# The last 64 channels of a channel product as 64-row tiles of the TensorE array

## The chip, the cores and the metric

The kernel runs on one core of one Trainium2 chip. The metric is the device time of one execution in microseconds (us), lower is better. TensorE is called PE below, VectorE DVE, ScalarE ACT, as in the profile's rows.

## What is computed

The reference first forms a small causal weighted sum over seven neighbours of each sequence position, with softmax weights per head, and then a mixer of two products: one over the sequence (tokens) and one over the channels. The part that the change touches is the channel part, at its end:

```
x   = weighted sum of 7 taps                       # [8, 4096, 192]
h   = relu(x.T @ w_tok1) @ w_tok2                  # token mixing
u   = x + h.T
out = u + relu(u @ w_ch1) @ w_ch2                  # 192 -> 1536 -> 192 channels
```

There are 8 batches of 4096 positions with 192 channels. `x` and the softmax weights arrive in single precision, the four mixer weights in double, and the result is single precision.

## The kernel before

The 32768 positions are worked in 64 groups of N = 512 positions, eight groups to a batch. A group `g` passes through `u` (positions as partitions), is transposed to channels as partitions, and then goes through six steps `p` of the channel part, each of which handles 256 of the 1536 features.

**Precision by two parts.** A single-precision factor is split into a rounded part (`hi`) and the rest (`lo`), and a product is formed as hi x hi + lo x hi + hi x lo in a fast one-pass format. The 192 channels are the rows of the first channel product `u @ w_ch1`. 128 of them (the `a` part) fill all rows of the array and need three matmuls: `w1a_hi` with `a_hi`, `w1a_lo` with `a_hi`, `w1a_hi` with `a_lo`. The last 64 (the `c` part) are stacked: the tile `uc` holds the rounded part in rows 0 to 63 and the rest in rows 64 to 127, and `w1c_hi` and `w1c_lo` hold the same 64 rows of weights twice. Two matmuls (L496) do the `c` part of one block of 128 features. So `channel1` issues, for each of the two feature blocks `j` of a step, five matmuls of 512 columns into one bank of `ph`.

**One step.** `channel1(g, p)` issues those ten matmuls, then `nc.scalar.activation` (L499, ACT) writes the rounded relu to `h`, and `scalar_tensor_tensor` (L500, DVE) its rest. `channel2` issues sixteen matmuls (L514, L516) on the `h` of two steps earlier, which accumulate over the six steps. `ph` shares a pool of two buffers (`ps_w`) with the results of the token matmuls `th` and `up`, so a `channel1` waits until the L500 of an earlier step has read its buffer.

**What stands between.** Within the steps of group `g` the kernel places the token matmuls of a later group (`do_token1`) and those that make `u` of group `g + 1` (`do_token2`, in two halves). After the second half, `columns_of` turns `u` around: one DVE transpose of 32 x 32 blocks (L468), 24 ACT copies of 32 rows each (L476) into `a_f` and `c_f`, and then `split_u`: ACT writes `a_hi` and rows 0 to 63 of `uc`, DVE subtracts for `a_lo` (L426) and for rows 64 to 127 of `uc` (L429). When the last of these has been issued, `ut[g + 1]` is set and the group may begin.

**What sets the order.** Each engine's queue is in the order in which the Python code issues. DVE and ACT have other work beside: the weighted sum (`attention`, L200 and L208, 13 DVE operations per group until the last batch), the softmax, and in the first batches the conversion of weights. This work stands in chains of items, each with a kind and a cost in ns. `pump` picks the next item with a small planner clock for each engine (`at`). A "v" item goes to DVE when its chain's due time allows, and of two that could start, a later chain is preferred only if it starts over 100 ns earlier. After a "v" item its chain waits 130 ns (`AFTER`), so that an item of another chain gets in between. "u" items (the copies of `columns_of` and `split_u`) go first, but only if they end by `max(at["pe"], w_at[0]) + C1 + LATE`. `C1` and `C2` are the planner's prices for `channel1` and `channel2` on PE, `TOP` that of L499. A chain is strictly serial: an item that may not be issued holds up all items behind it. If `ut[g + 1]` isn't set at the end of a group, `need` issues what is left and moves the planner's PE clock on by 500 ns a time.

**Start.** A prologue of 130 us converts the weights of the channel part and the first token weights from double precision and does the first batch's taps. The conversion of the `c` weights (`convert_channel`, which "w1c") splits them into a scratch tile `prk` and then makes eight ACT copies of 64 rows x 768 (L369) to write both halves of `w1c_hi` and `w1c_lo`.

Of the kernel before, what the change touches and what calls it, by code (L numbers as in the profile page):

```python
# [12 lines left out]
F32 = mybir.dt.float32  # L13
F32R = mybir.dt.float32r
# [7 lines left out]
def mixer_kernel(ctx: ExitStack, tc: tile.TileContext, x, wg, wt1, wt2, wc1, wc2, out):  # L22
    nc = tc.nc
    B, S, D = x.shape
# [20 lines left out]
    const = ctx.enter_context(tc.tile_pool(name="const", bufs=1))  # L45
# [12 lines left out]

    w1a_hi = const.tile([P, F], F32R, name="w1a_hi")
    w1a_lo = const.tile([P, F], F32R, name="w1a_lo")  # L60
    w1c_hi = const.tile([P, F], F32R, name="w1c_hi")
    w1c_lo = const.tile([P, F], F32R, name="w1c_lo")
    w2s = const.tile([P, NF, 2 * D], F32R, name="w2s")
    s0 = dram.tile([NCH, P, CT * R], F32, name="s0")
    s1 = dram.tile([NCH, P, CT * 2 * R], F32, name="s1")
# [42 lines left out]
    def raw_tile():  # L108

        n = staged["raw"]  # L110
        staged["raw"] += 1
        if pro is not None and n % 3 == 0:
            return pro.tile([P, NV, 2], U32, tag="raw", name="raw")
        tag = "w1" if (n - n // 3 - 1 if pro is not None else n + 1) % 2 else "raw"
        return p1.tile([P, NV, 2], U32, tag=tag, name="raw")
# [13 lines left out]
    def convert(raw, n, out):  # L129

        yield "gate", 0, lambda: state["vals"] < 2
        state["vals"] += 1
        v = val_tile()[:, 0:n]
        out.append(v)
        bits = v.bitcast(U32)
        low, high = raw[:, 0:n, 0], raw[:, 0:n, 1]
        act, stt = nc.scalar.activation, nc.vector.scalar_tensor_tensor
        yield "s", 950, lambda: act(v, high.bitcast(F32), AF.Abs)
        yield "s", 1050, lambda: act(v, v, AF.Sign, bias=below[:, 0:1])
        yield "s", 950, lambda: act(v, v, AF.Relu, scale=LOW30)  # L140
        cost = 70 + n * 1.05
        yield "v", cost, lambda: stt(bits, high, 3, bits, op0=ALU.logical_shift_left, op1=ALU.bitwise_and)
        yield "v", cost, lambda: stt(bits, low, 29, bits, op0=ALU.logical_shift_right, op1=ALU.bitwise_or)
        yield "v", cost, lambda: stt(bits, high, 0xC0000000, bits, op0=ALU.bitwise_and, op1=ALU.bitwise_or)

    def split(hi, lo, v):

        n = v.free_size()
        yield "a", 190 + n * 0.75, lambda: nc.scalar.copy(hi, v)
        yield "v", 70 + n * 1.05, lambda: nc.vector.tensor_sub(lo, v, hi.bitcast(F32))  # L150
# [81 lines left out]
    KA = 4  # L232
# [98 lines left out]
    HF = F // 2  # L331
    NF2 = NF // 3

    def fetch_channel(which, n):
        raw = raw_tile()
        if which == "w1a":
            cs = slice(2 * n * HF, 2 * (n + 1) * HF)
            nc.sync.dma_start(raw[:, 0:HF, :].rearrange("p n l -> p (n l)"), wc1[0:DA, cs])
        elif which == "w1c":
            for j in range(2):  # L340
                cs = slice(2 * j * HF, 2 * (j + 1) * HF)
                nc.sync.dma_start(raw[j * DC:(j + 1) * DC, 0:HF, :].rearrange("p n l -> p (n l)"), wc1[DA:D, cs])
        else:
            nc.sync.dma_start(
                raw[:, 0:NF2 * D, :].rearrange("p (f d) l -> p f (d l)", f=NF2),
                wc2[n * NF2 * P:(n + 1) * NF2 * P].rearrange("(f p) d -> p f d", p=P),
            )
        rawt[which, n] = raw

    def convert_channel(which, n, pool=None):  # L350
        out = []
        yield from convert(rawt.pop((which, n)), NF2 * D if which == "c2" else HF, out)
        yield "n", 0, lambda: raw_free()
        v, = out
        if which == "w1a":
            cs = slice(n * HF, (n + 1) * HF)
            yield from split(w1a_hi[:, cs], w1a_lo[:, cs], v)
        elif which == "c2":
            fs = slice(n * NF2, (n + 1) * NF2)
            yield from split(w2s[:, fs, 0:D], w2s[:, fs, D:2 * D], v.rearrange("p (f d) -> p f d", f=NF2))  # L360
        else:
            two = pool.tile([P, KA, CT, D], F32, tag="pr", name="prk", bufs=3)
            two = two.rearrange("p k t d -> p (k t d)").bitcast(F32R)
            hi, lo = two[:, 0:HF], two[:, HF:2 * HF]
            yield from split(hi, lo, v)
            for src, dst in ((hi, w1c_hi), (lo, w1c_lo)):
                for j in range(2):
                    for at in (0, DC):
                        yield "a", 730, lambda src=src, dst=dst, j=j, at=at: nc.scalar.copy(  # L369
                            dst[at:at + DC, j * HF:(j + 1) * HF], src[j * DC:(j + 1) * DC, :].bitcast(F32))  # L370

        def last():
            state["vals"] -= 1
            done.add((which, n))
        yield "n", 0, last
# [42 lines left out]
    ut = {}  # L418

    def split_u(m, a_f, c_f):  # L420
        a_hi = late.tile([P, N], F32R, tag="a_hi", name="a_hi", bufs=2)
        a_lo = late.tile([P, N], F32R, tag="a_lo", name="a_lo", bufs=2)
        uc = late.tile([P, N], F32R, tag="uc", name="uc", bufs=2)
        yield "u", 520, lambda: nc.scalar.copy(a_hi, a_f)  # L424
        yield "u", 520, lambda: nc.scalar.copy(uc[0:DC], c_f[0:DC])
        yield "v", 540, lambda: nc.vector.tensor_sub(a_lo, a_f, a_hi.bitcast(F32))  # L426

        def last():
            nc.vector.tensor_sub(uc[DC:P], c_f[0:DC], uc[0:DC].bitcast(F32))  # L429
            ut[m] = (a_hi, a_lo, uc)  # L430
        yield "v", 540, last

    Q = 32
    NQ = P // Q
# [52 lines left out]

    def channel1(g, p):

        a_hi, a_lo, uc = ut[g]  # L490
        ph = ps_w.tile([P, 2, 512], F32, tag="w", name="ph")
        steps = ((w1a_hi, a_hi), (w1a_lo, a_hi), (w1a_hi, a_lo), (w1c_hi, uc), (w1c_lo, uc))
        for j in range(2):
            fs = slice((2 * p + j) * P, (2 * p + j + 1) * P)
            for n, (w, u) in enumerate(steps):
                nc.tensor.matmul(ph[:, j, :], w[:, fs], u, start=n == 0, stop=n == len(steps) - 1)  # L496
        h = late.tile([P, 2, 2, N], F32R, tag="h", name="h", bufs=3)
        ht[g, p] = h
        nc.scalar.activation(h[:, :, 0, :], ph, AF.Relu)  # L499
        nc.vector.scalar_tensor_tensor(  # L500
            h[:, :, 1, :], ph, 0.0, h[:, :, 0, :].bitcast(F32), op0=ALU.max, op1=ALU.subtract
        )
# [32 lines left out]
    at = {"pe": 0.0, "act": 0.0, "dve": 0.0}  # L535
# [6 lines left out]
    SLACK_M = 400  # L542
    LATE = 300
    FIRST = 0
    C1, C2 = 2290, 2264
    TOP, LOW = 1040, 1135
    h_at, w_at, h1_at = {}, deque([0.0, 0.0]), {0: 0.0}
    free = {"acc": 0.0, "u": 0.0}
# [92 lines left out]
    def raw_free():  # L641

        if state["jobs"]:
            job, *what = state["jobs"].popleft()
            fetch_w2(*what) if job is convert_w2 else fetch_channel(*what)
            add_chain(job(*what), max(at["pe"], at["dve"]) + LOAD if at["pe"] > 0 else SOON)
# [29 lines left out]
    with tc.tile_pool(name="pro", bufs=1) as pro:  # L676
# [29 lines left out]
        for m in range(NCH):  # L706
# [3 lines left out]
            v, = w1_v.pop(m)  # L710
            current, channel = channel, None
            if m in between:
                fetch_channel(*between[m])
                channel = start(convert_channel(*between[m], pro))
            if m + 2 < NCH:
                start_w1(m + 2)
            elif m + 2 == NCH:
                fetch_w2(0)
                w2_it = start(convert_w2(0))
            else:  # L720
                fetch_channel("c2", 1)
                channel = start(convert_channel("c2", 1))
                fetch_channel("w1a", 1)
# [23 lines left out]
    late = ctx.enter_context(tc.tile_pool(name="late", bufs=1))  # L747
# [122 lines left out]
```

## Time and profile before

| | |
|---|---|
| median of 3 runs | 2344.61 us (2344.28 to 2345.2) |
| the profiled execution | 2343.91 us |
| its span in the profile | 2342.1 us |
| mean granted PE clock | 0.978 |

The profile is that of one execution. Its rows give the start and the length of instructions in us; a matmul's length includes the time in which its last columns pass through the array, so successive matmuls overlap in the rows and the step from one start to the next tells the pace. "Windows" are rows that give the busy time of each engine within a stretch of the span; a number in brackets after a row of the timeline is the idle time of the engine before it and what ended that. The lines themselves stand in the prediction.

### The profile page before, as it was taken

To read this page: it belongs to the slowest core of one execution; us is meant where nothing else is said; L and a number is where in the kernel's file an instruction comes from. 1 tells how busy PE (TensorE), PEld (TensorE's weight loads), DVE (VectorE), ACT (ScalarE), POOL (GpSimd) and SP (SyncE) were. 2 spreads that over 40 slices of the span, in tenths; PEclk is the share of its full clock that TensorE was granted. 3 is DMA by queue.
4 is the path that set the end of the run, shared out by engine and by line. 5 is a ranking of instruction groups with operands and counts; after the bars stand their busy time and mean duration, and the time that the engine had idled before them with its cause. 6 is when DMAs were issued, how large, how long until landed. Compare 5 with 4: busy or idle time off the path is not lost.

```text
span 2342.1 us, 30675 instructions
## 1 busy us (share of the span) xinstructions
PE 2196.7 (94%) x12256; PEld 1962.0 (84%) x12256; DVE 1842.1 (79%) x2231; ACT 1085.0 (46%) x2265; POOL 58.4 (2%) x104
## 2 busy tenths in 40 slices
PE   7869989999998999999999999999999999999998
PEld 5558878888887888888888888888888888899997
DVE  8889887878876888879887888869887798844443
ACT  4675443544534355345434434444443454344443
POOL 0000000000000000000000000000000000000000
PEclk9989999999999999999999999999999999999999
DMA  7733131223241333313332232332233132211110
GB/s 282 233 133 140 63 106 70 100 97 114 92 156 62 108 113 135 120 64 124 123 107 99 105 122 80 116 112 104 101 107 120 63 124 103 73 55 46 46 42 21
DMA packets 52127, 244.69 MB, mean 104 GB/s; under 512 B 6008, under 2 KB 15736, under 8 KB 38672
## 3 DMA queue, kind: packets, MB, share of 16 engines
q1 hardware_dynamic: 43360, 196.58, 24.3%
q0 software_dynamic: 8624, 46.14, 4.9%
q8 instruction: 97, 1.59, 0.3%
q14 instruction: 46, 0.38, 0.0%
HBM read 192.36 MB, written 50.33 MB: 104 GB/s over the span
## 4 chain that ended last, share of the span: by engine, by line
PE 38%; ACT 19%; DVE 14%; issue 11%; DMA 1%; POOL 0%; POOLq 0%; ACTq 0%; SPq 0%; DVEq 0%
PE ph L496 17%; ACT a_f L476 9%; PE acc L514 9%; ACT c_f L476 4%; PE acc L516 4%; ACT h L499 4%; DVE h L500 3%; DVE xa L208 3%; PE th L397 3%; DVE pr L200 3%; PE up L449 2%; DVE uc L429 1%; PE th L398 1%; DVE a_lo L426 1%; DMA w<-s 1%
## 5 line engine op out<-in xcount | busy, mean ns | idle before, releaser
L514 PE MATMUL acc<-w2s,h 128*128 128x384 f32 x3072 | 902.1, 358 | 0.0
L499 ACT ACTIVATE h<-ph 128x1024 fp32r<-128x1024 f32 x384 | 392.8, 1023 | 1004.4 <-PE ph L496 980.3
L516 PE MATMUL acc<-w2s,h 128*128 128x192 f32 x3072 | 773.5, 252 | 0.0
L500 DVE SCALAR_TENSOR_TENSOR h<-ph,h 128x1024 fp32r<-128x1024 f32 x384 | 468.3, 1220 | 294.3 <-ACT h L499 292.7
L516 PEld LDWEIGHTS acc<-w2s,h 128*128 128x128 f32 x3072 | 591.3, 192 | 16.0
L514 PEld LDWEIGHTS acc<-w2s,h 128*128 128x128 f32 x3072 | 583.3, 190 | 16.0
L496 PE MATMUL ph<-a_hi,w1a_hi 128*128 128x512 f32 x768 | 321.6, 419 | 58.9 <-ACT a_hi L424 33.9
L496 PE MATMUL ph<-uc,w1c_hi 128*128 128x512 f32 x768 | 311.7, 406 | 44.2 <-DVE uc L429 44.2
L200 DVE TENSOR_TENSOR pr<-xt,wn 128x768 f32<-128x768 f32 x336 | 318.2, 952 | 4.1
L208 DVE TENSOR_TENSOR xa<-xa,pr 128x768 f32<-128x768 f32 x336 | 319.7, 952 | 1.0
L496 PE MATMUL ph<-a_lo,w1a_hi 128*128 128x512 f32 x768 | 306.8, 399 | 6.0 <-DVE a_lo L426 6.0
L476 ACT COPY a_f<-t 32x128 f32<-32x128 f32 x1024 | 302.6, 295 | 16.6 <-DVE t L468 5.5
L496 PE MATMUL ph<-a_hi,w1a_lo 128*128 128x512 f32 x768 | 305.6, 398 | 0.0
L496 PE MATMUL ph<-uc,w1c_lo 128*128 128x512 f32 x768 | 305.2, 397 | 0.0
L496 PEld LDWEIGHTS ph<-uc,w1c_hi 128*128 128x128 f32 x768 | 146.6, 191 | 97.6 <-DVE uc L429 49.4
L496 PEld LDWEIGHTS ph<-a_hi,w1a_hi 128*128 128x128 f32 x768 | 146.5, 191 | 87.4 <-ACT a_hi L424 37.3
L496 PEld LDWEIGHTS ph<-a_lo,w1a_hi 128*128 128x128 f32 x768 | 146.6, 191 | 45.8 <-DVE a_lo L426 14.4
L496 PEld LDWEIGHTS ph<-uc,w1c_lo 128*128 128x128 f32 x768 | 147.4, 192 | 30.1
L496 PEld LDWEIGHTS ph<-a_hi,w1a_lo 128*128 128x128 f32 x768 | 148.0, 193 | 16.0
L476 ACT COPY c_f<-t 32x128 f32<-32x128 f32 x512 | 152.0, 297 | 7.4
L528 DVE TENSOR_TENSOR ur<-acc,ur 128x384 f32<-128x384 f32 x256 | 136.2, 553 | 8.3 <-PE acc L516 3.9
L449 PE MATMUL up<-h,w 128*128 128x384 f32 x384 | 116.4, 359 | 0.0
(70 smaller groups left out, 1914.8 us busy)
## 6 DMA issues: line engine op xcount, KB each, us to landing
w<-s SPq DMA_DIRECT2D x80, 1024.0 KB
xt<-in_x_dram SPq DMA_DIRECT2D x56, 960.0 KB
out_dram<-ur POOLq DMA_DIRECT2D x63, 384.0 KB, 4.9
raw<-in_moe_w_tok_dram SPq DMA_DIRECT2D x16, 1024.0 KB
s<-w POOLq DMA_DIRECT2D x16, 1024.0 KB, 4.1
val<-s SPq DMA_DIRECT2D x24, 512.0 KB
wg<-in_weight_gen_dram SPq DMA_DIRECT2D x64, 112.0 KB
s<-val SPq DMA_DIRECT2D x8, 512.0 KB
```

What stands on the lines that cost most here:

```text
L200: nc.vector.tensor_mul(dst.rearrange("p t (h g) -> p (t h) g", h=H).rearrange("p (o n) g -> p o n g", o=1), x_k, w)
L208: nc.vector.tensor_add(box["acc"], box["acc"], box.pop(k))
L397: nc.tensor.matmul(th[:, r, 0:2 * D], w[:, c, 0, rs], xh[:, c, :], start=c == 0, stop=False)
L398: nc.tensor.matmul(th[:, r, 0:D], w[:, c, 1, rs], xh[:, c, 0:D], start=False, stop=c == CT - 1)
L449: nc.tensor.matmul(up[:, j, 0:2 * D], w[:, k, 0, cs], h1[:, k, :], start=k == 0, stop=False)
L476: nc.scalar.copy(dst[to:to + Q, :].rearrange("p (c n j) -> p c n j", c=CT, n=NQ)[:, :, n, :], box["t"][n * Q:(n + 1) * Q, :, d, :])
L496: nc.tensor.matmul(ph[:, j, :], w[:, fs], u, start=n == 0, stop=n == len(steps) - 1)
L499: nc.scalar.activation(h[:, :, 0, :], ph, AF.Relu)
L500: nc.vector.scalar_tensor_tensor(h[:, :, 1, :], ph, 0.0, h[:, :, 0, :].bitcast(F32), op0=ALU.max, op1=ALU.subtract)
L514: nc.tensor.matmul(ps[:, 0:2 * D], h[:, j, 0, cs], w2s[:, f, :], start=f == 0, stop=False, **kw)
L516: nc.tensor.matmul(ps[:, 0:D], h[:, j, 1, cs], w2s[:, f, 0:D], start=False, stop=f == NF - 1, **kw)
L528: nc.vector.tensor_add(u[:, t, :], a[:, :, l * D:(l + 1) * D], u[:, t, :])
```

## The change

`uc` becomes two tiles. `c_hi` holds the rounded part of the last 64 channels in rows 0 to 63 and again in rows 64 to 127, `c_lo` the rest in the same way. The weights `w1c_hi` and `w1c_lo` are half as long: rows 0 to 63 hold the 64 weight rows of even feature blocks and rows 64 to 127 those of odd ones. The two feature blocks of a step are then done by two matmuls of 64 rows, one on rows 0 to 63 of the array and one on rows 64 to 127, each into its own bank of `ph`; three such pairs replace the four matmuls of 128 rows. The order within a step changes too: first the six `a` matmuls of both blocks, then the pairs.

`split_u` has two more ACT copies and another order. The conversion of the `c` weights writes its result in place and has no scratch tile and no L369 copies; the load of the raw weights fetches pieces of 128 numbers (1 KB) where it fetched rows of 768 numbers (6 KB). The planner's price `C1` goes from 2290 to 2250.

```
-    w1c_hi = const.tile([P, F], F32R, name="w1c_hi")
-    w1c_lo = const.tile([P, F], F32R, name="w1c_lo")
+    w1c_hi = const.tile([P, F // 2], F32R, name="w1c_hi")
+    w1c_lo = const.tile([P, F // 2], F32R, name="w1c_lo")
...
             for j in range(2):
-                cs = slice(2 * j * HF, 2 * (j + 1) * HF)
-                nc.sync.dma_start(raw[j * DC:(j + 1) * DC, 0:HF, :].rearrange("p n l -> p (n l)"), wc1[DA:D, cs])
+                nc.sync.dma_start(
+                    raw[j * DC:(j + 1) * DC, 0:HF, :].rearrange("p (q n) l -> p q (n l)", q=NP),
+                    wc1[DA:D].rearrange("c (q j n) -> c q j n", q=NP, j=2)[:, :, j, :])
...
-            two = pool.tile([P, KA, CT, D], F32, tag="pr", name="prk", bufs=3)
-            two = two.rearrange("p k t d -> p (k t d)").bitcast(F32R)
-            hi, lo = two[:, 0:HF], two[:, HF:2 * HF]
-            yield from split(hi, lo, v)
-            for src, dst in ((hi, w1c_hi), (lo, w1c_lo)):
-                for j in range(2):
-                    for at in (0, DC):
-                        yield "a", 730, lambda src=src, dst=dst, j=j, at=at: nc.scalar.copy(
-                            dst[at:at + DC, j * HF:(j + 1) * HF], src[j * DC:(j + 1) * DC, :].bitcast(F32))
+            yield from split(w1c_hi, w1c_lo, v)
...
-        uc = late.tile([P, N], F32R, tag="uc", name="uc", bufs=2)
+        c_hi = late.tile([P, N], F32R, tag="c_hi", name="c_hi", bufs=2)
+        c_lo = late.tile([P, N], F32R, tag="c_lo", name="c_lo", bufs=2)
+        yield "u", 520, lambda: nc.scalar.copy(c_hi[0:DC], c_f[0:DC])
         yield "u", 520, lambda: nc.scalar.copy(a_hi, a_f)
-        yield "u", 520, lambda: nc.scalar.copy(uc[0:DC], c_f[0:DC])
+        yield "u", 520, lambda: nc.scalar.copy(c_hi[DC:P], c_f[0:DC])
+        yield "v", 540, lambda: nc.vector.tensor_sub(c_lo[0:DC], c_f[0:DC], c_hi[0:DC].bitcast(F32))
         yield "v", 540, lambda: nc.vector.tensor_sub(a_lo, a_f, a_hi.bitcast(F32))
 
         def last():
-            nc.vector.tensor_sub(uc[DC:P], c_f[0:DC], uc[0:DC].bitcast(F32))
-            ut[m] = (a_hi, a_lo, uc)
-        yield "v", 540, last
+            nc.scalar.copy(c_lo[DC:P], c_lo[0:DC].bitcast(F32))
+            ut[m] = (a_hi, a_lo, c_hi, c_lo)
+        yield "u", 520, last
...
-        steps = ((w1a_hi, a_hi), (w1a_lo, a_hi), (w1a_hi, a_lo), (w1c_hi, uc), (w1c_lo, uc))
         for j in range(2):
             fs = slice((2 * p + j) * P, (2 * p + j + 1) * P)
-            for n, (w, u) in enumerate(steps):
-                nc.tensor.matmul(ph[:, j, :], w[:, fs], u, start=n == 0, stop=n == len(steps) - 1)
+            for n, (w, u) in enumerate(((w1a_hi, a_hi), (w1a_lo, a_hi), (w1a_hi, a_lo))):
+                nc.tensor.matmul(ph[:, j, :], w[:, fs], u, start=n == 0, stop=False)
+        for n, (w, u) in enumerate(((w1c_hi, c_hi), (w1c_lo, c_hi), (w1c_hi, c_lo))):
+            for j in range(2):
+                rows = slice(j * DC, (j + 1) * DC)
+                nc.tensor.matmul(ph[:, j, :], w[rows, p * P:(p + 1) * P], u[rows], start=False, stop=n == 2)
...
-    C1, C2 = 2290, 2264
+    C1, C2 = 2250, 2264
```

More of the change, by code (lines that the diff above doesn't have):

```diff
@@ L488, in channel1 @@
     def channel1(g, p):
-        a_hi, a_lo, uc = ut[g]
+        a_hi, a_lo, c_hi, c_lo = ut[g]
         ph = ps_w.tile([P, 2, 512], F32, tag="w", name="ph")
-        steps = ((w1a_hi, a_hi), (w1a_lo, a_hi), (w1a_hi, a_lo), (w1c_hi, uc), (w1c_lo, uc))
         for j in range(2):
             fs = slice((2 * p + j) * P, (2 * p + j + 1) * P)
-            for n, (w, u) in enumerate(steps):
-                nc.tensor.matmul(ph[:, j, :], w[:, fs], u, start=n == 0, stop=n == len(steps) - 1)
+            for n, (w, u) in enumerate(((w1a_hi, a_hi), (w1a_lo, a_hi), (w1a_hi, a_lo))):
[4 more added lines that the diff above has]
+                nc.tensor.matmul(ph[:, j, :], w[rows, p * P:(p + 1) * P], u[rows], start=False, stop=n == 2)
         h = late.tile([P, 2, 2, N], F32R, tag="h", name="h", bufs=3)
```

## The prediction

> **What bounds the kernel now.** I read the page first, then the windows by group, then the timeline where one group follows another.
>
> ```profile
> span 2342.1 us, 30675 instructions
> ...
> PE 2196.7 (94%) x12256; PEld 1962.0 (84%) x12256; DVE 1842.1 (79%) x2231; ACT 1085.0 (46%) x2265; POOL 58.4 (2%) x104
> ```
>
> PE is busy in 94% of the span, but the windows show two regimes.
>
> ```profile
> core 0: us, PE busy (x) PEld busy (x) DVE busy (x) ACT busy (x) POOL busy (x), PEclk, DMA share, GB/s
> 459.39:493.34 33.95, 32.87 (x191) 29.71 (x189) 27.23 (x33) 15.97 (x35) 1.08 (x2) 1.00 0.29 110
> 493.34:636.86 143.52, 134.36 (x755) 121.78 (x753) 115.72 (x141) 64.79 (x139) 5.36 (x9) 0.98 0.28 101
> 1107.55:1241.32 133.77, 129.77 (x755) 117.57 (x753) 114.93 (x145) 60.63 (x135) 3.21 (x5) 1.00 0.31 108
> 2092.46:2299.48 207.02, 207.02 (x1207) 190.28 (x1205) 98.45 (x121) 98.79 (x225) 3.78 (x7) 1.00 0.12 45
> ```
>
> The last row holds groups 56 to 62, counted from group 0 at the first `channel1`: 207.02 / 7 = 29.57 us a group, PE busy all the time, DVE half idle. There, what PE saves is saved. The row above it holds groups 27 to 30, 133.77 / 4 = 33.44 us each, with DVE busy 28.7 us of it. What they have beyond the token work of the other row is waits of PE:
>
> ```profile
> 1207.79 0.25 PE L516 MATMUL acc<-w2s,h 128*128 128x192 f32 x1
> 1207.88 0.41 PE L496 MATMUL ph<-a_hi,w1a_hi 128*128 128x512 f32 x1
> 1208.13 0.40 PE L496 MATMUL ph<-a_hi,w1a_lo 128*128 128x512 f32 x1
> 1208.36 0.40 PE L496 MATMUL ph<-a_lo,w1a_hi 128*128 128x512 f32 x1
> 1209.03 0.50 PE L496 MATMUL ph<-uc,w1c_hi 128*128 128x512 f32 x1 [0.27 <-DVE uc L429]
> 1209.36 0.40 PE L496 MATMUL ph<-uc,w1c_lo 128*128 128x512 f32 x1
> 1209.60 0.39 PE L496 MATMUL ph<-a_hi,w1a_hi 128*128 128x512 f32 x1
> 1209.83 0.39 PE L496 MATMUL ph<-a_hi,w1a_lo 128*128 128x512 f32 x1
> ```
>
> Three numbers come out of it. A 512-column matmul steps 0.23 us (1209.60 to 1209.83) though its row lasts 0.39, so 0.16 is a tail that the next one covers. One whose weights couldn't be loaded ahead lasts 0.50, and the next starts 0.33 later: a cold weight load costs 0.10. And `uc`, due at 1208.59, starts at 1209.03: each group begins with a wait on DVE. A second wait comes later in the group, on a `ph` buffer:
>
> ```profile
> 1215.02 0.50 PE L496 MATMUL ph<-a_hi,w1a_hi 128*128 128x512 f32 x1 [0.74 <-DVE h L500]
> ```
>
> **The pairs on PE.** Per step four matmuls of 128 rows go, 4 x 0.23, and three pairs of 64 rows come. Call what a step saves s. No row shows two tiles side by side, so I bound s. If the second of a pair rides free beside the first, three paces replace four: s = 0.23. If it trails by one weight load: s = 0.13. If also the first load on each side of the pairs can't be made ahead, two cold loads go off: s = -0.07. If PE must also run empty at both changes, two tails of 0.16 go off: s = -0.39. If the tiles don't overlap, six paces replace four: s = -0.46. I take 0.03, midway between the second and the third, since the cold load is the one such cost that rows show.
>
> The page "TensorE: Matmul & The Clock Gate" of the Trainium skill (Part 3, Packing small matmuls) says that tiles on different row groups run side by side at some 4 ns a tile; by that s would be near 0.23 and the sum that of the first rival below. Its page "TensorEngine Tiling (Array Packing)" (Key Properties) speaks against the change: switching the tiling mode drains the engine; by that alone s would be 0.23 less two tails, -0.09, and the sum 2378. No row here shows either.
>
> How much of s reaches the end? In groups 56 to 63 all six steps of a group, about 7.5 x 6 = 45 s. In some 35 regular groups before them, DVE's order sets the group's first wait and the wait on L500; behind that PE runs steps 1 to 3 without a wait, to the L499 that the ACT copies for the next group follow, so three steps count: 105 s. DVE doesn't bind in that stretch, it waits there for PE:
>
> ```profile
> 1227.87 0.56 DVE L456 TENSOR_TENSOR ur<-up,xa 128x384 f32<-128x384 f32 x1 [0.45 <-PE up L450]
> ```
>
> For the other groups I count nothing. Together 150 s: -4.5 us at 0.03, from -34 (s = 0.23) to +58 (s = -0.39).
>
> **`split_u`, where the order holds.** The end of group 30 on ACT, DVE and PE:
>
> ```profile
> 1239.48 0.62 ACT L424 CAST a_hi<-a_f 128x512 fp32r<-128x512 f32 x1
> 1240.01 0.61 ACT L425 CAST uc<-c_f 64x512 fp32r<-64x512 f32 x1
> 1240.53 1.02 ACT L499 ACTIVATE h<-ph 128x1024 fp32r<-128x1024 f32 x1
> ```
>
> ```profile
> 1240.13 0.69 DVE L426 TENSOR_TENSOR a_lo<-a_f,a_hi 128x512 fp32r<-128x512 f32 x1 [0.41 <-ACT a_hi L424]
> 1240.74 0.95 DVE L208 TENSOR_TENSOR xa<-xa,pr 128x768 f32<-128x768 f32 x1
> 1241.73 0.69 DVE L429 TENSOR_TENSOR uc<-c_f,uc 64x512 fp32r<-64x512 f32 x1
> 1242.44 1.23 DVE L500 SCALAR_TENSOR_TENSOR h<-ph,h 128x1024 fp32r<-128x1024 f32 x1
> ```
>
> ```profile
> 1241.32 0.41 PE L496 MATMUL ph<-a_hi,w1a_hi 128*128 128x512 f32 x1
> ...
> 1241.80 0.40 PE L496 MATMUL ph<-a_lo,w1a_hi 128*128 128x512 f32 x1
> ```
>
> ACT now does `c_hi` first, so `a_hi` ends near 1240.63, still 0.69 before PE wants it. The second `c_hi` copy pushes L499 back by 0.52, to end near 1242.07, before DVE takes L500 at 1242.44. On DVE `c_lo` takes the place of `a_lo`, a tap operation follows (130 ns of `AFTER` against 100), and `a_lo` takes the place of `uc`, ready at the same 1242.42. PE wants `a_lo` as its third matmul, one pace before it wanted `uc`: the wait grows by 0.23, and the later one on L500 swallows that. The `c_lo` copy follows L499 and ends near 1242.7; its pair comes over 1 us after `a_lo`. So nothing here. The two copies more are 64 x 2 x 0.61 = 78 us of ACT, hidden in an engine that is 46% busy; without that cover the one ahead of `a_hi` would cost 63 x 0.52 = 33 us.
>
> **`split_u`, where the order breaks.** By the planner's sums in ns, from its end of `channel1` of step 3: L499 ends at 1100 (HOP + TOP); nine moves of 400 fit below 2264 + 2250 + 300 = 4814, which makes 4700. L499 of step 4 brings 5740, three moves 6940, three copies of 520 then 8500; the limit is 2 x 2250 + 2 x 2264 + 300 = 9328. All fit. But 16 times an L149 copy, priced 958, falls in such a group, most often among the moves:
>
> ```profile
> L149 ACT CAST w<-val 128x1024 fp32r<-128x1024 f32 x16 | 16.7, 1047 | 0.2
> ```
>
> Then the third copy would end at 9458, 130 too late, where before the second and last ended at 8938 below 9408. It is held back behind `channel1` of step 5, and with it, the chain being serial, both subtractions: they follow L500 of step 5. The trace shows what one subtraction behind L500 does, at the end of group 10:
>
> ```profile
> 531.37 1.22 DVE L500 SCALAR_TENSOR_TENSOR h<-ph,h 128x1024 fp32r<-128x1024 f32 x1
> 532.61 0.69 DVE L429 TENSOR_TENSOR uc<-c_f,uc 64x512 fp32r<-64x512 f32 x1
> ```
>
> ```profile
> 533.44 0.47 PE L496 MATMUL ph<-uc,w1c_hi 128*128 128x512 f32 x1 [2.29 <-DVE uc L429]
> ```
>
> In the windows above, group 9 is begun without this and takes 33.95; groups 10 to 13 are begun with it and take 143.52 / 4 = 35.88, their granted clock at 0.98: 1.93 us a group. Afterwards the order would be L500, `c_lo`, a tap operation, `a_lo`: `a_lo` 0.6 + 1.0 later than `uc` was, and wanted 0.23 sooner. Per broken start the cost lies between 0.2 (only the earlier want) and 4 (from a start without to two behind); I take the measured 1.9. How many? Of the 16, by their due times, ten keep so little room; of the first seven groups, with conversions in between, I count two. 12 x 1.9 = 23 us, from 2 to 48.
>
> **The prologue.** Eight copies leave ACT:
>
> ```profile
> 100.36 3.35 ACT L369 CAST w1c_hi<-prk 64x768 fp32r<-64x768 f32 x4
> 103.72 3.36 ACT L369 CAST w1c_lo<-prk 64x768 fp32r<-64x768 f32 x4
> ...
> 112.13 2.07 ACT L303 COPY w<-val 128x1024 f32<-128x1024 f32 x1
> ...
> 116.64 0.47 ACT L381 ACTIVATE h<-th 128x384 f32<-128x384 f32 x1
> ```
>
> ```profile
> 107.50 1.23 DVE L144 SCALAR_TENSOR_TENSOR val<-raw,val 128x1024 uint32<-128x1024 uint32 x1
> ```
>
> They take 6.7 us, and ACT stays nearly full up to L381, from which the first group's `u` follows. L303 needs the L144 that ends at 108.73, so the queue can move up 112.13 - 108.73 = 3.4 us: I take -3, between -6.7 and +3 (the raw load in 1 KB pieces may land later; it is asked for one round of the loop ahead). The scratch tile's place frees a buffer that no row waits for.
>
> **The sum**, against the profiled execution's 2343.9 (its span 2342.1 and 1.8 around it): -3 - 4.5 + 23 = +15.5, so 2359.4; the median shown is 0.7 higher: **2360**. Its own range, from 4 to 18 broken starts and s from 0.13 to -0.07, is 2330 to 2386.
>
> **The rivals.**
> - *The pairs pack well*, s = 0.23: -34 - 3 + 23 = -14, 2330; faster. It decides from 150 s = 20, s = 0.13, on, which is the trailing case. For it: weight loads lie beside matmuls everywhere in the rows. Against: no row shows a change of tiles without a cost. Chance 0.30.
> - *The order stays*: few starts break, 3 x 1.9: -4.5 - 3 + 6, 2343. For it: the limit is missed by only 130 ns, and the planner's clock is moved by every wait in `need`. Against: the sum above. Chance 0.14.
> - *PE runs empty at each change of tiles*, s = -0.39 (or tiles in turn, -0.46): +58 + 23 - 3 = +78, 2422 to 2433. For it: the tail of 0.16 is in every row. Against: the change of shape from L516 to L496 (1207.79 to 1207.88) shows none. The drain that "TensorEngine Tiling (Array Packing)" of the Trainium skill states belongs here. Chance 0.12.
>
> **How the numbers follow.** The forecast keeps 0.44. A measurement of this kernel can tell some 0.2%, 4.7 us, from no change. Faster: 0.30 of the first rival and 0.06 of the second, 0.36. Same: 0.07 of the second and 0.03 of the forecast's lower edge, 0.10. Slower: the rest, 0.54. The range takes in the first rival with fewer broken starts, 2318, and above the forecast's range s = -0.19, 2395; it leaves out the drain and a few more.
>
> **What would show it.** Right: starts of `channel2` after `channel1` about 0.03 earlier in groups 56 to 62, so 29.4 us a group; `a_lo` behind L500 at the starts of groups 9 to 14, with waits of PE near 4 us; groups 27 to 30 within 0.2 of 33.44; the first `channel1` near 127. Wrong: groups 56 to 62 at 28.2 (packing) or 31.9 (running empty), or groups 9 to 14 no longer than 36.

## The result, and the profile after

| | before | after | ratio (95% interval) |
|---|---|---|---|
| median of 4 runs each (lowest to highest), us | 2344.45 (2342.27 to 2345.2) | 2450.35 (2447.11 to 2454.13) | 1.0454 (1.0434 to 1.0474) |
| span of the profiled execution, us | 2342.1 | 2445.3 | |
| mean granted PE clock | 0.978 | 0.964 | |

The kernel became slower by 106 us. The prediction said slower, by 15.5 us. The sign was right, the size was not, and the time lies outside the range.

The first lines of the page of the changed kernel:

```profile
span 2445.3 us, 32227 instructions
...
PE 2283.5 (93%) x13024; PEld 1847.2 (76%) x13024; DVE 1842.4 (75%) x2231; ACT 1160.1 (47%) x2385; POOL 58.4 (2%) x104
```

The span grew by 103.2 us. PE was busy for 86.8 of these and idle for 16.4: mostly, PE's own work became longer. Weight loads became shorter in sum, 1847.2 against 1962.0. The windows of the same groups as before (9, 10 to 13, 27 to 30, 56 to 62) show where the time went:

```profile
core 0: us, PE busy (x) PEld busy (x) DVE busy (x) ACT busy (x) POOL busy (x), PEclk, DMA share, GB/s
470.66:509.36 38.70, 35.24 (x202) 28.92 (x201) 27.33 (x32) 17.24 (x37) 1.08 (x2) 0.96 0.26 96
509.36:666.09 156.73, 142.91 (x802) 116.26 (x801) 115.52 (x140) 69.74 (x147) 5.37 (x9) 0.93 0.26 92
1168.88:1303.89 135.01, 133.78 (x802) 109.81 (x801) 114.51 (x145) 65.98 (x143) 3.21 (x5) 1.00 0.31 107
2186.15:2401.55 215.40, 215.40 (x1291) 176.38 (x1289) 97.76 (x120) 109.04 (x240) 3.78 (x7) 1.00 0.13 43
```

Two different losses stand side by side. The last row is PE alone: 215.40 / 7 = 30.77 us a group against 29.57, so a step became 1.20 / 6 = 0.20 longer. The second row is something else: 156.73 / 4 = 39.18 a group against 35.88, with a granted clock of 0.93 against 0.98. The third row, where the order holds, grew only from 33.44 to 33.75.

**One step on PE**, from the timeline of the changed kernel (start, length; x2 is a pair):

```profile
2203.86 0.39 PE L492 MATMUL ph<-a_lo,w1a_hi 128*128 128x512 f32 x1
2204.18 0.50 PE L496 MATMUL ph<-c_hi,w1c_hi 64*128 64x512 f32 x2
2204.51 0.40 PE L496 MATMUL ph<-c_hi,w1c_lo 64*128 64x512 f32 x2
2204.74 0.40 PE L496 MATMUL ph<-c_lo,w1c_hi 64*128 64x512 f32 x2
2205.07 0.44 PE L514 MATMUL acc<-w2s,h 128*128 128x384 f32 x1
2205.35 0.25 PE L516 MATMUL acc<-w2s,h 128*128 128x192 f32 x1
```

The pairs do ride side by side: a pair lasts 0.40, as one matmul does, and the next comes 0.23 later (2204.51 to 2204.74); in the records of one pair the second tile starts 3 ns after the first. The loss is at the edges. The first pair starts 0.32 after the last full matmul, not 0.23: 0.09 late. It lasts 0.50 and the next pair starts 0.33 later: one cold load of 0.10. At the way out L514 starts 0.33 after the last pair, again 0.10 late, and L516 follows it by 0.28, where full_rows below has 0.17 in the same place: another cold load. The pairs save one pace, 0.23, and the two edges cost some 0.4. The weight loads (PEld) of the first pair and of L514 begin together with their matmuls:

```profile
2204.17 0.19 PEld L496 LDWEIGHTS ph<-c_hi,w1c_hi 64*128 64x128 f32 x2 [0.35 <-issue]
...
2205.07 0.19 PEld L514 LDWEIGHTS acc<-w2s,h 128*128 128x128 f32 x1 [0.37 <-issue]
```

In full_rows the load for the same place (L513 there) begins 0.22 ahead of its matmul, which starts at 2178.57:

```profile
2178.35 0.19 PEld L513 LDWEIGHTS acc<-w2s,h 128*128 128x128 f32 x1
```

**One start of a group.** Group 9 begins at 470.66. ACT, DVE and PE around it, one fence each:

```profile
470.37 1.02 ACT L499 ACTIVATE h<-ph 128x1024 fp32r<-128x1024 f32 x1
471.41 0.62 ACT L421 CAST c_hi<-c_f 64x512 fp32r<-64x512 f32 x1
```

```profile
471.42 1.23 DVE L500 SCALAR_TENSOR_TENSOR h<-ph,h 128x1024 fp32r<-128x1024 f32 x1 [0.80 <-ACT h L499]
472.56 0.67 DVE L422 TENSOR_TENSOR c_lo<-c_f,c_hi 64x512 fp32r<-64x512 f32 x1
473.16 0.94 DVE L200 TENSOR_TENSOR pr<-xt,wn 128x768 f32<-128x768 f32 x1
474.03 0.68 DVE L423 TENSOR_TENSOR a_lo<-a_f,a_hi 128x512 fp32r<-128x512 f32 x1
```

```profile
474.76 0.50 PE L492 MATMUL ph<-a_lo,w1a_hi 128*128 128x512 f32 x1 [3.46 <-DVE a_lo L423]
```

This is the sequence that the prediction wrote down: the third copy (L421) behind L499 of step 5, then L500, `c_lo`, a tap, `a_lo`, and PE waits 3.46 us. What follows the wait on PE had not been written down:

```profile
477.99 0.57 PE L514 MATMUL acc<-w2s,h 128*128 128x384 f32 x1
478.36 0.36 PE L516 MATMUL acc<-w2s,h 128*128 128x192 f32 x1
478.52 0.57 PE L514 MATMUL acc<-w2s,h 128*128 128x384 f32 x1
...
479.55 0.36 PE L514 MATMUL acc<-w2s,h 128*128 128x384 f32 x1
...
479.83 0.36 PE L514 MATMUL acc<-w2s,h 128*128 128x384 f32 x1
```

L514 and L516 together take 0.53 (477.99 to 478.52) and from 479.55 on 0.28: the same matmuls at half speed. By the same timeline the slow stretch begins with the pairs at 475.89 and ends near 479.4, so 3.5 us of it, in which some 1.7 us are lost. This wait is paid twice.

### The profile page after: what moved, and what is told of

Same layout as the page of the kernel before. It is cut to its first block, busy times and chain, and to the rows that moved or that the text cites. A ratio compares the mean times of both kernels' runs of the same rounds, so it can differ in the third digit from the quotient of the medians.

```text
span 2445.3 us, 32227 instructions
## 1 busy us (share of the span) xinstructions
PE 2283.5 (93%) x13024; PEld 1847.2 (76%) x13024; DVE 1842.4 (75%) x2231; ACT 1160.1 (47%) x2385; POOL 58.4 (2%) x104
## 4 chain that ended last, share of the span: by engine, by line
PE 38%; issue 29%; ACT 19%; DVE 12%; DMA 1%; POOL 1%; SPq 0%; POOLq 0%; ACTq 0%; DVEq 0%
PE ph L492 10%; PE acc L514 9%; ACT a_f L473 8%; PE ph L496 7%; ACT h L499 4%; PE acc L516 4%; ACT c_f L473 3%; DVE h L500 3%; PE th L391 2%; DVE pr L200 2%; DVE xa L208 2%; PE up L444 2%; PE up L446 2%; DVE prk L240 1%; PE th L392 1%
## 5 line engine op out<-in xcount | busy, mean ns | idle before, releaser
L514 PE MATMUL acc<-w2s,h 128*128 128x384 f32 x3072 | 951.0, 374 | 0.0
L499 ACT ACTIVATE h<-ph 128x1024 fp32r<-128x1024 f32 x384 | 393.2, 1024 | 996.0 <-PE ph L496 994.9
L516 PE MATMUL acc<-w2s,h 128*128 128x192 f32 x3072 | 774.6, 252 | 0.0
L500 DVE SCALAR_TENSOR_TENSOR h<-ph,h 128x1024 fp32r<-128x1024 f32 x384 | 469.1, 1222 | 387.1 <-ACT h L499 384.2
L514 PEld LDWEIGHTS acc<-w2s,h 128*128 128x128 f32 x3072 | 584.6, 190 | 147.9 <-issue 133.2
L516 PEld LDWEIGHTS acc<-w2s,h 128*128 128x128 f32 x3072 | 594.7, 194 | 0.0
L492 PE MATMUL ph<-a_lo,w1a_hi 128*128 128x512 f32 x768 | 318.5, 415 | 72.9 <-DVE a_lo L423 72.9
L496 PE MATMUL ph<-c_hi,w1c_hi 64*128 64x512 f32 x768 | 199.7, 516 | 0.0
L496 PEld LDWEIGHTS ph<-c_hi,w1c_hi 64*128 64x128 f32 x768 | 74.3, 190 | 145.1 <-issue 145.1
L496 PE MATMUL ph<-c_hi,w1c_lo 64*128 64x512 f32 x768 | 159.1, 411 | 0.0
L496 PE MATMUL ph<-c_lo,w1c_hi 64*128 64x512 f32 x768 | 158.5, 408 | 0.2 <-ACT c_lo L426 0.2
L391 PE MATMUL th<-xh,w 128*128 128x384 f32 x384 | 114.6, 363 | 3.4 <-DVE ur L528 2.9
```

The costliest lines, as they stand in the source:

```text
L391: nc.tensor.matmul(th[:, r, 0:2 * D], w[:, c, 0, rs], xh[:, c, :], start=c == 0, stop=False)
L496: nc.tensor.matmul(ph[:, j, :], w[rows, p * P:(p + 1) * P], u[rows], start=False, stop=n == 2)
L500: nc.vector.scalar_tensor_tensor(h[:, :, 1, :], ph, 0.0, h[:, :, 0, :].bitcast(F32), op0=ALU.max, op1=ALU.subtract)
L514: nc.tensor.matmul(ps[:, 0:2 * D], h[:, j, 0, cs], w2s[:, f, :], start=f == 0, stop=False, **kw)
L516: nc.tensor.matmul(ps[:, 0:D], h[:, j, 1, cs], w2s[:, f, 0:D], start=False, stop=f == NF - 1, **kw)
```

## The experiments

Each is the changed kernel with the edit shown, unless "before" is said. In the table of sections the time of the profiled execution is cut at the first `channel1` of a group; groups 0 to 7 are the first batch, and the last 11 us of the span, after group 63, are alike in all. The times of the text are medians of all runs, and the sums of the table can differ from them by some us.

| us | to group 0 | groups 0 to 7 | 8 to 23 | 24 to 54 | 55 to 63 | starts at which PE is idle over 1.5 us before an `a_lo` matmul, or in the kernels with `uc` before one of `uc` or `a_lo` |
|---|---|---|---|---|---|---|
| before | 129.7 | 296.0 | 581.1 | 1053.7 | 270.7 | 9 |
| after | 128.3 | 308.4 | 623.4 | 1093.0 | 281.3 | 23 |
| full_rows | 129.7 | 306.9 | 615.3 | 1076.7 | 270.7 | 23 |
| limit_off | 129.3 | 311.1 | 598.3 | 1092.6 | 281.3 | 17 |
| a_lo_first | 130.8 | 298.4 | 592.3 | 1083.1 | 281.3 | 0 |
| full_rows_a_lo_first | 129.2 | 297.7 | 583.5 | 1058.8 | 270.7 | 0 |
| true_price | 127.9 | 302.7 | 604.9 | 1061.8 | 281.3 | 13 |
| true_price_a_lo_first | 129.7 | 297.1 | 576.5 | 1082.0 | 281.3 | 0 |
| limit_off_a_lo_first | 130.1 | 296.9 | 576.7 | 1080.6 | 281.3 | 0 |
| before_by_factor | 130.0 | 294.6 | 567.5 | 1048.2 | 270.7 | 8 |

The theory after the first look: PE loses 0.2 us a step at the two changes of tile shape, and the rest of the loss is the order of `split_u`, by which `a_lo` falls behind an L500. The rival for the second part: the two more ACT copies, or something not yet seen, cost by themselves.

**full_rows: the pairs as four matmuls of 128 rows again**, on the tiles of the changed kernel.

```
-        for n, (w, u) in enumerate(((w1c_hi, c_hi), (w1c_lo, c_hi), (w1c_hi, c_lo))):
+        for n, (w, u) in enumerate(((w1c_hi, c_hi), (w1c_lo, c_lo))):
             for j in range(2):
-                rows = slice(j * DC, (j + 1) * DC)
-                nc.tensor.matmul(ph[:, j, :], w[rows, p * P:(p + 1) * P], u[rows], start=False, stop=n == 2)
+                nc.tensor.matmul(ph[:, j, :], w[:, p * P:(p + 1) * P], u, start=False, stop=n == 1)
```

> The changed kernel with its six 64-row matmuls per step replaced by four of 128 rows on the same tiles (the c part of the product is thereby computed wrongly); split_u, the prices and the order of all queues stay. Theory (most of the loss is the order at the starts of groups, the rest the pairs on PE): groups 56 to 62 return from 30.77 to 29.6 us each, the waits of 3.6 us on a_lo at the starts of groups 9 to 14 stay, 2390 to 2420 us. Rival (the pairs on PE are the whole loss, the waits follow from them): 2340 to 2355 us, and waits on a_lo under 1 us.

Measured 2409.46 us, ratio 1.0280 (1.0264 to 1.0295). The windows of groups 10 to 13 and 56 to 62 of this kernel:

```profile
508.43:662.33 153.90, 138.82 (x753) 124.97 (x753) 115.44 (x141) 69.76 (x147) 5.36 (x9) 0.94 0.26 94
2160.36:2367.37 207.01, 207.01 (x1206) 190.26 (x1205) 97.66 (x121) 109.64 (x240) 3.78 (x7) 1.00 0.13 45
```

The second row is before's to the hundredth: 29.57 a group. The first still has 38.5 a group. So the pairs cost 2450.35 - 2409.46 = 41 us, and the waits at the starts don't come from them. Its timeline of one step shows the same stretch without a change of shape:

```profile
2177.44 0.39 PE L492 MATMUL ph<-a_lo,w1a_hi 128*128 128x512 f32 x1
...
2178.57 0.33 PE L513 MATMUL acc<-w2s,h 128*128 128x384 f32 x1
2178.74 0.25 PE L515 MATMUL acc<-w2s,h 128*128 128x192 f32 x1
```

From the last `a` matmul to the 192-column one: 2178.74 - 2177.44 = 1.30, against 2205.35 - 2203.86 = 1.49 with pairs. The difference, 0.19, is the step's loss.

**four_switches: the first pair ahead of the two `a_lo` matmuls**, so that a step enters and leaves the 64-row shape twice.

```
...
+        full(0, w1a_hi, a_hi)
+        full(1, w1a_lo, a_hi)
+        pair(0, w1c_hi, c_hi)
+        full(2, w1a_hi, a_lo)
+        pair(1, w1c_lo, c_hi)
+        pair(2, w1c_hi, c_lo)
```

> The changed kernel with the first pair of each step moved ahead of the two a_lo matmuls, so that a step goes between full rows and 64-row tiles four times, not twice; nothing else changes. Theory (each change costs a late start of 0.1 us and a cold weight load of 0.1 us): a step takes 0.4 us more, groups 56 to 62 33.2 us each instead of 30.77. Rival (the pairs themselves are slow, whatever stands between): groups 56 to 62 stay at 30.8.

Measured 2495.45 us in one run. Its window of groups 56 to 62:

```profile
2214.88:2447.38 232.50, 232.50 (x1291) 172.91 (x1289) 97.38 (x120) 108.22 (x239) 3.77 (x7) 1.00 0.12 40
```

(`full` issues two matmuls of 128 rows, `pair` one pair; their definitions are left out above.) 232.50 / 7 = 33.21, as expected, with the same matmuls as at 30.77: one more way in and out costs 2.44 / 6 = 0.41 us. This prices the change of shape by itself, and with it the change's own step: 0.23 saved less 0.41 is -0.18, where -0.20 was measured. The total is not this price alone: `a_lo` is wanted later in this order, and the waits at groups 9 to 14 are 1.70 us here.

**limit_off: the copies of `split_u` may end 1500 ns later by the planner**, so that the third is not held back.

```
-                    end = max(at["pe"], w_at[0]) + C1 + LATE
+                    end = max(at["pe"], w_at[0]) + C1 + LATE + (1500 if c.item[1] == 520 else 0)
```

> The changed kernel, with 1500 ns added to the planner's limit for the copies of split_u alone, so that none is held back. Theory (held-back copies put a_lo behind L500 of step 5): no waits of over 1.5 us on a_lo at the starts of groups 9 to 14, 25, 26, 33 and 34, groups 56 to 62 unchanged at 30.77 us, 2365 to 2390 us. Rival (the pairs alone): 2440 us or more, since the pairs are as before.

Measured 2424.80 us, ratio 1.0343 (1.0327 to 1.0358): better than the change by 26 us, but 35 above the upper end of what the theory expected. Groups 10 to 13 are cured:

```profile
508.92:647.33 138.41, 134.80 (x803) 110.97 (x801) 115.33 (x142) 70.21 (x147) 5.35 (x9) 1.00 0.29 105
```

But 17 starts still wait. Group 25 in this kernel, on ACT, DVE and PE:

```profile
1071.78 0.62 ACT L421 CAST c_hi<-c_f 64x512 fp32r<-64x512 f32 x1
1072.42 1.02 ACT L499 ACTIVATE h<-ph 128x1024 fp32r<-128x1024 f32 x1
```

```profile
1071.27 0.96 DVE L200 TENSOR_TENSOR xa<-xt,wn 128x768 f32<-128x768 f32 x1
1072.15 0.68 DVE L422 TENSOR_TENSOR c_lo<-c_f,c_hi 64x512 fp32r<-64x512 f32 x1
1072.75 0.94 DVE L200 TENSOR_TENSOR pr<-xt,wn 128x768 f32<-128x768 f32 x1
1073.62 1.21 DVE L500 SCALAR_TENSOR_TENSOR h<-ph,h 128x1024 fp32r<-128x1024 f32 x1
1074.76 0.67 DVE L423 TENSOR_TENSOR a_lo<-a_f,a_hi 128x512 fp32r<-128x512 f32 x1
```

```profile
1075.48 0.50 PE L492 MATMUL ph<-a_lo,w1a_hi 128*128 128x512 f32 x1 [2.40 <-DVE a_lo L423]
```

Here no copy is held back: L421 stands ahead of L499. `c_lo` is due one copy later than the first subtraction was in before, a tap goes ahead of it, `AFTER` puts another behind it, and `a_lo`, the second in a serial chain, no longer fits ahead of L500. In before the same start had both subtractions and one tap between them ahead of L500:

```profile
1039.57 0.69 DVE L426 TENSOR_TENSOR a_lo<-a_f,a_hi 128x512 fp32r<-128x512 f32 x1
1040.18 0.95 DVE L200 TENSOR_TENSOR xa<-xt,wn 128x768 f32<-128x768 f32 x1
1041.16 0.69 DVE L429 TENSOR_TENSOR uc<-c_f,uc 64x512 fp32r<-64x512 f32 x1
1041.88 1.23 DVE L500 SCALAR_TENSOR_TENSOR h<-ph,h 128x1024 fp32r<-128x1024 f32 x1
```

So there is a second way to the same wait, and the theory of the copy limit alone falls.

**full_rows_limit_off: both edits.**

> Both of these edits together (the c part is again computed wrongly). Theory (two separate causes that add up): 2335 to 2350 us, groups 56 to 62 at 29.6 us, no long waits on a_lo. Rival (something else in the change costs, such as the two more ACT copies or the prologue's load): 2365 us or more.

Measured 2382.00 us, ratio 1.0164 (1.0147 to 1.0181). The theory had before's time within some us, the rival 2365 or more: the rival (something else in the change costs) fits, though most of it is neither of the two candidates that it named, as the runs with `a_lo` first show below. 38 us were still unexplained at this point, and the starts with `a_lo` behind L500 without a held copy were the candidate. The next experiment goes at these.

**a_lo_first: the same six operations in another order**: what PE wants first is made first.

```
         yield "u", 520, lambda: nc.scalar.copy(c_hi[0:DC], c_f[0:DC])
         yield "u", 520, lambda: nc.scalar.copy(a_hi, a_f)
-        yield "u", 520, lambda: nc.scalar.copy(c_hi[DC:P], c_f[0:DC])
-        yield "v", 540, lambda: nc.vector.tensor_sub(c_lo[0:DC], c_f[0:DC], c_hi[0:DC].bitcast(F32))
         yield "v", 540, lambda: nc.vector.tensor_sub(a_lo, a_f, a_hi.bitcast(F32))
+        yield "v", 540, lambda: nc.vector.tensor_sub(c_lo[0:DC], c_f[0:DC], c_hi[0:DC].bitcast(F32))
+        yield "u", 520, lambda: nc.scalar.copy(c_hi[DC:P], c_f[0:DC])
```

> The changed kernel with the items of split_u in another order: copies of c_hi (upper rows) and a_hi, then the subtractions a_lo and c_lo, then the two copies to the lower rows. Nothing is left out. Theory (two ways lead to the loss at group starts: a third copy that misses the limit, and a_lo as the later of two subtractions, which a tap operation and L500 overtake; both go, and c_lo isn't wanted before the pairs): no waits of over 1 us on a_lo, 2360 to 2380 us, which is before plus the pairs' 1.2 us in the last nine groups and 0.3 to 0.5 in the regular ones. Rival (the planner's limit for copies is all of it): about as the run with that limit raised, 2415 to 2430 us.

Measured 2392.53 us, ratio 1.0218 (1.0201 to 1.0234): 58 us better than the change, 12 above what the theory had said at most, and far from the rival. At group 10 `a_lo` comes in time, and it is now `c_lo`, wanted last, that stands behind an L500:

```profile
499.94 0.51 PE L492 MATMUL ph<-a_lo,w1a_hi 128*128 128x512 f32 x1
...
502.52 0.49 PE L496 MATMUL ph<-c_lo,w1c_hi 64*128 64x512 f32 x1 [0.71 <-DVE c_lo L422]
```

A wait of 0.71 instead of 3.4: `a_lo` is the third matmul of a step, `c_lo` belongs to the last pair, and the matmuls between cover the rest.

**full_rows_a_lo_first: this order, with full rows.** It keeps both additional ACT copies and the changed prologue, and takes away the two suspected causes.

> The changed kernel without the pairs (four matmuls of 128 rows in their place, so that the c part is computed wrongly) and with a_lo as the first subtraction, as in the run a_lo_first; limit and price as in the change. Theory (pairs, limit and the place of a_lo are the whole loss, and with a_lo first a copy that misses the limit no longer stops PE's third matmul): 2335 to 2360 us, groups 27 to 30 at 33.3 to 33.5 us. Rival (the two more ACT copies cost by themselves): 2365 us or more.

Measured 2347.38 us, ratio 1.0015 (1.0006 to 1.0025): as expected, before's time within 4 us. Groups 27 to 30 came to 134.88 / 4 = 33.72, above the expected 33.3 to 33.5. The windows of groups 10 to 13 and 27 to 30 of this kernel:

```profile
496.27:636.02 139.75, 132.38 (x752) 118.58 (x753) 115.00 (x141) 69.77 (x147) 5.38 (x9) 1.00 0.29 104
1111.56:1246.44 134.88, 129.78 (x754) 117.58 (x753) 114.17 (x146) 65.58 (x143) 3.22 (x5) 1.00 0.31 107
```

ACT has some 5 us more work in each row than before had, and the time shows little of it. The four corners close the account, in ratios to the runs of before beside them:

| | order of the change | `a_lo` first |
|---|---|---|
| pairs of 64 rows | 1.0454 | 1.0218 |
| full rows | 1.0280 | 1.0015 |

The pairs cost 1.7% or 2.0% (41 or 45 us), the order 2.4% or 2.7% (58 or 62 us), and what is left over is 0.15%. That rest is a net: it holds the two ACT copies, the prologue and the later place of the `c` part in a step, which before_by_factor below prices alone; the runs don't part it further.

**true_price: `C1` = 2460** instead of 2250, near what a step with pairs takes.

> The changed kernel with C1 at 2460, what ten matmuls' successor takes by the profile (4.74 less 2.28 us), instead of 2250. Theory (the limit of the copies is missed because the planner believes a step shorter than it is): starts of groups 9 to 14 without waits of 3.6 us, 2400 to 2430 us, since the other way to lose remains. Rival (the price of C1 doesn't matter): 2440 to 2455.

Measured 2391.22 us in one run, better than either theory had it, and not where the theory had it. Groups 24 to 54 come down from 1093.0 to 1061.8, and none of their starts waits over 1.5 us for `a_lo` any more; that a later due time on PE leaves room for both subtractions ahead of L500 is argued from the planner's sums, not shown. Groups 9 to 14, which the theory had cured, still wait 2.7 to 2.8 us each.

**true_price_a_lo_first** and **limit_off_a_lo_first**: the repaired order with each of the two planner edits, to see whether the pairs can win at all.

> The changed kernel with the pairs, C1 at 2460 and a_lo as the first subtraction: its form with the order repaired in both ways. Theory (what is left is the pairs' cost on PE, 10.7 us in the last nine groups and under 0.5 us in each other): 2350 to 2375 us, still slower than before. Rival (with the order repaired the pairs cost nothing that shows): 2335 to 2349 us.

> The changed kernel with 1500 ns more of the planner's limit for the copies of split_u and a_lo as the first subtraction, C1 at 2250. Theory (a_lo first helps alone, the limit is then of little weight): within 15 us of the 2392 of a_lo_first. Rival (both add up as price and place do): 2350 to 2375 us.

Measured 2379.08 us, ratio 1.0143 (1.0126 to 1.0160), 4 above the expected stretch, and 2378.29 us in one run. That is 14 below the 2392 of a_lo_first, just inside the theory's 15 and 3 above its rival's stretch, so it decides little between the two. Both are slower than before. With the order as good as these planner edits make it, the pairs still cost more than they save: even the best sections that the runs with pairs reached, each from its own run and put together (127.9, 296.9, 576.5, 1061.8, 281.3 and the last 11), come to 2355 us against before's span of 2342.1.

**before_by_factor: before, with the ten matmuls ordered by factor.** The change also put the `a` matmuls of both blocks ahead of the `c` part, so that the part that is ready last is wanted last. This kernel does so on before's tiles:

```
-        for j in range(2):
-            fs = slice((2 * p + j) * P, (2 * p + j + 1) * P)
-            for n, (w, u) in enumerate(steps):
+        for n, (w, u) in enumerate(steps):
+            for j in range(2):
+                fs = slice((2 * p + j) * P, (2 * p + j + 1) * P)
```

> The kernel before, with the ten matmuls of a step ordered by factor, both feature blocks for each, so that uc is wanted as the seventh and a_lo as the fifth; the same matmuls, no pairs. Theory (part of the starts of groups is PE waiting for the last subtraction; wanted 0.69 us later, the waits of 1.3 and 2.6 us on uc shrink by up to that, and in the regular groups L500 takes the gain back): 2325 to 2340 us, groups 56 to 62 unchanged at 29.57. Rival (DVE sets the pace of the regular and the early groups whatever PE wants first): 2342 to 2347.

Measured 2325.16 us, ratio 0.9929 (0.9914 to 0.9944): the fastest of all but its own variant below. Windows of groups 10 to 13 and 27 to 30:

```profile
492.18:629.89 137.71, 130.24 (x755) 118.88 (x753) 115.34 (x141) 64.86 (x139) 5.36 (x9) 1.00 0.29 105
1091.18:1224.93 133.75, 128.61 (x755) 117.89 (x753) 114.86 (x145) 60.65 (x135) 3.21 (x5) 1.00 0.32 108
```

The regular groups stay at 33.44: what `uc` gains at the start, the wait on L500 takes back. Groups 10 to 13 fall from 143.52 to 137.71 and their clock rises from 0.98 to 1.00. `uc` is wanted as the seventh matmul and not the fourth, so the wait at group 10 is 1.87 and not 2.29:

```profile
495.62 0.70 PE L496 MATMUL ph<-uc,w1c_hi 128*128 128x512 f32 x2 [1.87 <-DVE uc L429]
```

In before these groups went by turns, as its windows of groups 10 and 11 show:

```profile
493.34:530.01 36.67, 34.38 (x190) 31.19 (x189) 30.54 (x39) 16.43 (x36) 1.08 (x2) 0.95 0.26 96
530.01:565.08 35.07, 32.78 (x191) 29.70 (x189) 27.32 (x33) 15.97 (x35) 1.08 (x2) 1.00 0.28 106
```

Both begin with the same wait on `uc`, but only the first has a stretch at half speed (its granted clock is 0.95), and it takes 1.6 us longer; with the wait at 1.87 every group from 10 to 13 takes 34.4 to 34.5, at a clock of 1.00.

**before_by_factor_limit_off**: that kernel with the later limit for the copies.

> The same with 1500 ns more of the planner's limit for the copies of split_u. Theory (in before, too, some copies are held back, at groups 14, 16 and 17 alone by the due times): 0 to 8 us below the run without it. Rival: the shifted order costs elsewhere, up to 10 us above.

Measured 2324.04 us, ratio 0.9924 (0.9907 to 0.9940): no different from the one above.

## Why the prediction had the sign and not the size

**s, the saving of a step: mis-sized.** Taken as +0.03, measured -0.20. The cases were right in kind: the pairs ride free (the 0.23 of the best case), and cold loads go off on both sides. The step that failed is "midway between the second and the third, since the cold load is the one such cost that rows show": it put all costs of the pairs at 0.20, which is the two cold loads alone; a late start at a change of shape was put at nothing. The row that it set against such a loss, L516 to L496 in before, changes the number of columns and not that of rows. The trace shows none inside the pairs, but at each change of shape a whole cold load and a late start of 0.09 to 0.10 besides, 0.41 for both: 0.23 - 0.41 = -0.18. PE does not run empty by the rows: the late start is less than the tail of 0.16. The value lies between the third case and the fourth; the prediction had it only as the upper edge of its range, s = -0.19 (for which its own terms give 2393, not the 2395 that it states).

The page "TensorEngine Tiling (Array Packing)" of the Trainium skill (Key Properties) says that a change of tiling mode drains the engine; the trace agrees in part: each change costs 0.09 to 0.10, but the first pair starts 0.07 before the row of the last full matmul ends (2204.18 against 2203.86 + 0.39), and the loads that were not made ahead come on top. The 4 ns a tile of "TensorE: Matmul & The Clock Gate" (Part 3) agree with the 3 ns within a pair; the page's rule describes the inside of such a stretch, and the loss is at its edges.

**How much of s reaches the end: too little.** I counted 150 steps; 41 us at 0.20 are 205. (The profiled executions of after and full_rows, which the sections cut up, lie 35 apart, the medians 41.) By the sections of after and full_rows, groups 55 to 63 pay 10.6 (281.3 - 270.7), 24 to 54 pay 16.3, or 0.53 a group and so 2.6 steps, near the three that I took. But groups 0 to 23, of which the prediction counted only some ("for the other groups I count nothing"), pay 1.5 + 8.1.

**Where the order holds: right.** Groups 27 to 30 came to 33.75, and to 33.33 in full_rows, by the starts of its groups. The wait on `a_lo` is swallowed as said; the extra 0.4 is the pairs, and by it the forecast's sign "within 0.2 of 33.44" was missed.

**Where the order breaks: right in mechanism, wrong in count and price.** This is the second large error: 23 us against 58 to 62, beside -4.5 against 41 to 45 for the pairs. The count failed in taking the missed limit, "130 too late", as the sole way: groups begun with a long wait are 23, where before had 9 and I counted 12 that break, because the later due time of `c_lo` breaks groups in which all copies fit. I looked at group 30 only, where both subtractions do fit. The price failed at "I take the measured 1.9": that was the mean of 36.67 and 35.07, one subtraction behind L500, half of the groups followed by half speed. The prediction's own sum said that `a_lo` would come 1.6 later than `uc` did and be wanted 0.23 sooner, which leads to its upper bound of 4. Groups 9 to 14 grew by 4.8, 1.9, 4.7, 1.9, 4.7 and 2.9, the smaller numbers where before had its stretch at half speed already.

How much of the order's cost is the clock? full_rows and full_rows_a_lo_first have the same matmuls. Their spans are 2410.0 and 2350.8; the next lines of their pages, full_rows first:

```profile
PE 2226.5 (92%) x12256; PEld 1989.9 (83%) x12256; DVE 1841.4 (76%) x2231; ACT 1160.7 (48%) x2385; POOL 58.4 (2%) x104
```

```profile
PE 2198.6 (94%) x12256; PEld 1961.9 (83%) x12256; DVE 1832.5 (78%) x2231; ACT 1156.1 (49%) x2385; POOL 58.6 (2%) x104
```

The spans differ by 59.2, the busy times of PE by 27.9. Nearly half of the price of this order is not idle time of PE but slower matmuls: the mean granted clock is 0.961 in full_rows and 0.978 in the other.

**The prologue: right in sign, small.** Group 0 starts at 128.3 rather than 129.7, -1.4 against -3. But over the kernels of the table with the changed prologue it lies between 127.9 and 130.8, so this says little.

**ACT's 78 us of copies: hidden where PE alone sets the pace, elsewhere not shown.** full_rows_a_lo_first has them and takes before's time within 0.15%, but as a net with the later `c` part. before_by_factor has a later `c` part too, and against it full_rows_a_lo_first is 0.9% slower, some 20 us. In the sections of the profiled executions, which lie 29 apart, none of this is in groups 55 to 63, 16 are in groups 8 to 23 and 11 in 24 to 54. The two also differ in when `a_lo` is wanted and `c_lo` is made, so how much of this the copies cost stays open.

## What to carry to other kernels

A pair of small tiles must save more than the way into that shape and out of it costs, here 0.4 us, so one saved matmul of 0.23 us a visit doesn't pay; gathering more of the work in one shape into one visit is the way that suggests itself, and it was not tried here. Put first what the consumer wants first, and when an item in a serial chain is delayed, check the item behind it against its next obstacle, at several places of the schedule and not at one. Behind a wait look for a slow stretch, and price the two together.

## What was not expected of the hardware

- The weight load of the first matmul after a change between 128 and 64 rows is not made ahead, in either direction; together with the late start a round trip cost 0.41 us (30.77 to 33.21 us a group for six more).
- In before_by_factor, waits of 1.87 us at the starts of groups 10 to 12 were followed by no slow stretch; in before, waits of 2.29 by one in every second group; in after, waits of about 3.4 in groups 9 to 14 by one each time. It lasted some 3.5 us at half speed, and about twice that in groups 11 and 13 of after (granted clock 0.91 against 0.96 in the others). "TensorE: Matmul & The Clock Gate" of the Trainium skill (Why this matters for your kernels) puts the bound at gaps of about 3 us; the trace of before has some at 2.29. The length of one wait does not decide it here: in a_lo_first groups 10 to 13 each begin with a wait of 0.71 to 0.73 on `c_lo`, and every second one has the slow stretch all the same. What decides which group is hit stays open. The windows of groups 11 and 12 of a_lo_first:

```profile
534.61:571.53 36.92, 36.04 (x203) 29.55 (x201) 27.22 (x33) 17.21 (x37) 1.08 (x2) 0.95 0.27 101
571.53:606.81 35.28, 34.40 (x202) 27.90 (x201) 30.33 (x39) 17.68 (x38) 2.13 (x3) 1.00 0.31 99
```
- Ordering before's matmuls by factor, with nothing computed otherwise, was worth 0.7%, though the wait that it shortened became only some 0.4 us shorter: most of the gain lies in groups 8 to 23 (567.5 us against 581.1), where the slow stretches of groups 10, 12 and 14 went.
